# Loading 216 extra weight rows with four plain two-dimensional transfers instead of one three-dimensional one

## The chip, the cores and the metric

The kernel runs on one core of one Trainium2 chip. The metric is the device time of one launch in microseconds (us). Each comparison below was run in rounds on one chip: the kernel under test and the kernel before in turn. Runs of the kernel before scatter between 1334.8 and 1335.7 us over the chips used, and within one set of rounds on one chip by 0.2 to 0.8 us, so a few tenths of a microsecond are at the edge of what can be seen.

## The reference, cut to what matters

Two branches work on the same two rows `x` (two batch rows, one position, 1024 wide). Branch A is attention over a long cache, branch B a small mixing network. The result is a gated sum.

```python
# A: 32 heads, 16384 cached positions, head size 128, bf16: 2 x 268 MB of cache are read once
q = (x @ wq) per head;  p = softmax(q @ k_cache^T * 128**-0.5);  a = (p @ v_cache) @ wo
# B
h  = gelu(layernorm(x) @ w1)
hs = shifted(h) @ w2            # shifts along the sequence, zero padded
x1 = x + hs;  b = x1 + gelu(layernorm(x1) @ w3) @ w4
out = g * a + (1 - g) * b
```

The sequence has one position, so every shifted block of `h` is padding: `shifted(h)` is all zeros and `hs` is zero. The kernel still loads all of `w2` (1024 x 1024 bf16, 2 MB) and multiplies it by a tile of zeros.

## The kernel before

K and V are loaded in 8 MB pieces (two heads each) into a ring of three buffers, always from the SP queue. The small weights take a turn in the same ring. `w1` and `w2` share one turn, issued about 204 us into the run.

```python
    WAYS, QUAD, BASE, MORE = 3, 4, 6, 18
    W2_MORE = slice(0, WAYS * QUAD)                      # partitions 0 to 11
    n_more = WAYS * QUAD * MORE                          # 216 rows, 432 KB
    n_rest = D - P * BASE - n_more                       # 40 rows
    W2_REST = slice(64, 64 + n_rest)
    W2_ROWS = ( [(slice(0, P), r) for r in range(BASE)]
        + [(W2_MORE, BASE + r) for r in range(MORE)]
        + [(W2_REST, BASE)] )

    def load_w1_w2():
        t = load_rows(["w1"], [B_w1])
        w2 = t[:, KC * D : (KC + BASE + MORE) * D].rearrange("p (r n) -> p r n", n=D)
        nc.sync.dma_start(                               # six rows on each of 128 partitions
            out=w2[:, 0:BASE, :], in_=B_w2[0 : P * BASE, :].rearrange("(p r) n -> p r n", p=P)
        )
        r0 = P * BASE
        nc.sync.dma_start(                               # 18 more rows on each of partitions 0 to 11
            out=w2[W2_MORE, BASE : BASE + MORE, :],
            in_=B_w2[r0 : r0 + n_more, :].rearrange("(y x r) n -> x y (r n)", x=WAYS, y=QUAD),
        )
        r0 += n_more
        nc.sync.dma_start(out=w2[W2_REST, BASE, :], in_=B_w2[r0:D, :])   # 40 rows
    # ... cut ...
    def half_rows(key, actT, slots):                     # one matmul per slot and half
        for n, (rows, r) in enumerate(slots):
            for g in range(2):
                nc.tensor.matmul(ps[group(g), :], lhsT=actT[rows, r, :],
                    rhs=w[rows, r, g * HW : (g + 1) * HW], ...)
```

So `w2` is not spread evenly: 256 of its rows are taken from the even share and 216 of them put on 12 partitions.

Of the kernel before, what the change touches and what calls it, by code (L numbers as in the profile page):

```python
# [23 lines left out]
def kernel(  # L24
# [15 lines left out]
    nc = tc.nc  # L40
# [84 lines left out]
    WAYS, QUAD, BASE, MORE = 3, 4, 6, 18  # L125
    W2_MORE = slice(0, WAYS * QUAD)
    n_more = WAYS * QUAD * MORE
# [9 lines left out]
# [3 lines that stand above are left out]
        nc.sync.dma_start(  # L140
            out=w2[:, 0:BASE, :], in_=B_w2[0 : P * BASE, :].rearrange("(p r) n -> p r n", p=P)
        )
        r0 = P * BASE
        nc.sync.dma_start(
            out=w2[W2_MORE, BASE : BASE + MORE, :],
            in_=B_w2[r0 : r0 + n_more, :].rearrange("(y x r) n -> x y (r n)", x=WAYS, y=QUAD),
        )
        r0 += n_more
        nc.sync.dma_start(out=w2[W2_REST, BASE, :], in_=B_w2[r0:D, :])
        wt["w2"] = w2  # L150

    def load_rows(keys, srcs):

        t = big_tile("wt")
        c0 = 0
        for key, src in zip(keys, srcs):
            R, N = src.shape[0] // P, src.shape[1]
            v = t[:, c0 : c0 + R * N].rearrange("p (r n) -> p r n", n=N)
            nc.sync.dma_start(out=v, in_=src.rearrange("(p r) n -> p r n", p=P))
            wt[key] = v  # L160
            c0 += R * N
        return t
# [18 lines left out]
    def load_first():  # L181
# [12 lines left out]
        out=perm[:].rearrange("k (h a) -> k h a", a=4),  # L194
        in_=ident_f[:].rearrange("k (a h) -> k h a", a=4),
# [26 lines left out]
    for g in range(1, 4):  # L222
        nc.vector.tensor_tensor(
            out=osel_f, in0=osel_f, in1=ident_f[:, 40 * g : 40 * g + 8], op=ALU.add
# [9 lines left out]
        out=pick[:], in_=ident_f[:].rearrange("p (g w) -> p g w", w=32)[:, :, 0:B]  # L234
# [395 lines left out]
    def st_down():  # L630
# [5 lines left out]

    extra = {
        NT // 8: (load_w1_w2, st_mix),
        NT // 4: (lambda: load_rows(["w3"], [B_w3]), st_up),
    }  # L640
# [44 lines left out]
    for b, queue in enumerate((nc.sync, nc.scalar)):  # L685
        queue.dma_start(
            out=out[b].rearrange("s (g n) -> (s g) n", g=NQ), in_=rows[b : 96 + b + 1 : 32, :]
# [31 lines left out]
```

## Time and profile before

| what | value | view |
|---|---|---|
| device time | 1334.93 us (1334.92 to 1335.04, 3 runs) | times |
| bytes from HBM | 572.5 MB, 429 GB/s over the span | queue part of the page |
| DMA engines busy | 99.4% on the one hardware queue | queue part of the page |
| PE / DVE busy | 60% / 57% | busy part of the page |
| a 64 KB packet of K or V on one engine | 2.418 us | packets in the trace |
| one K or V load (8 such packets per engine) | lands every 19.33 us, mid-run | semaphore landings in the trace |

From the page of the kernel before: busy time, the row of 40 slices for the DMA engines (tenths, 9 is 90% or more), what they moved, the queue of the loads and the one that brings instructions (packets, MB, share of 16 engines' span), and the chain of waits by engine.

```profile
PE 797.4 (60%) x4974; PEld 351.3 (26%) x5037; DVE 760.1 (57%) x999; ACT 27.2 (2%) x68; POOL 12.8 (1%) x40
...
DMA  9999999999999999999999999999999999999998
GB/s 410 437 439 417 439 431 437 423 433 433 438 432 435 429 427 439 439 437 427 429 437 431 439 431 439 429 431 437 429 435 433 439 431 429 435 432 437 429 422 338
...
q1 hardware_dynamic: 12729, 572.54, 99.4%
q8 instruction: 39, 0.64, 0.2%
...
DVE 30%; PE 30%; DMA 23%; another core or an unknown queue 12%; issue 2%; ACT 1%; SPq 0%; ACTq 0%
```

Two parts of this page seem to disagree. The chain of waits gives DVE and PE 30% each, but the DMA engines are never idle. The chain follows what released the *issue* of each load (a buffer that PE or DVE had to free). A load that is issued while others are still queued starts no earlier for being issued earlier: the extra rows are issued by 206.1 us, and their first packet starts at 243.4 us. Here the DMA row and the GB/s row decide: the kernel is bound by the transfers.

The second view is the timeline of SP, which issues the loads, around `w1` and `w2` (start, duration, queue and line, output from input). L159 is `w1`, L140 the six even rows, L144 the extra rows, L149 the 40 rows, L108 a K load and L119 a V load.

```profile
199.62 0.33 SPq L119 DMA_DIRECT2D Vn<-in_A_v_cache_dram  x1
204.37 0.33 SPq L159 DMA_DIRECT2D wt<-in_B_w_dram  x1
204.74 0.43 SPq L140 DMA_DIRECT2D wt<-in_B_w_dram  x1
205.22 0.91 SPq L144 DMA_DIRECT2D wt<-in_B_w_dram  x1
206.17 0.39 SPq L149 DMA_DIRECT2D wt<-in_B_w_dram  x1
238.22 0.35 SPq L108 DMA_DIRECT2D Kn<-in_A_k_cache_dram  x1
242.97 0.33 SPq L119 DMA_DIRECT2D Vn<-in_A_v_cache_dram  x1
258.40 0.33 SPq L108 DMA_DIRECT2D Kn<-in_A_k_cache_dram  x1
```

SP is idle between these lines. All four loads of `w1` and `w2` are issued by 206.6 us, and the data of the extra rows lands only at 249.7 to 249.9 us: they spend most of that in the queue behind V.

The third view is a table of busy time in short stretches of the same region. The last two columns are the mean busy share of the DMA engines and GB/s; in a short stretch the share can read over 1.00, and then it only says that packets were in flight throughout.

```profile
core 0: us, PE busy (x) PEld busy (x) DVE busy (x) ACT busy (x) POOL busy (x), PEclk, DMA share, GB/s
242.00:246.00 4.00, 1.88 (x26) 1.15 (x18) 1.86 (x7) 0.00 (x0) 0.00 (x0) 0.99 1.25 488
246.00:250.00 4.00, 2.75 (x14) 1.05 (x15) 2.21 (x11) 0.78 (x2) 0.70 (x1) 0.50 1.03 422
250.00:254.00 4.00, 4.00 (x25) 1.18 (x21) 1.23 (x2) 0.00 (x0) 0.00 (x0) 0.66 1.05 446
...
256.60:260.40 3.80, 3.02 (x38) 1.75 (x34) 1.22 (x2) 0.00 (x0) 0.00 (x0) 0.89 1.03 449
```

While the extra rows are moved (243 to 250 us) the rate stays above 420 GB/s.

### The profile page before, as it was taken

The page shows a single profiled execution, that of the slowest core. Times are in us where ns is not written, and L with a number is a line of the kernel's source. Part 1 is how long each engine was busy: PE and PEld are TensorE (multiplying, and loading weights), DVE is VectorE, ACT ScalarE, POOL GpSimd, SP SyncE. Part 2 cuts the span into 40 slices and gives each one's busy share as a digit, 9 for nine tenths or more (in the row PEclk, how much of TensorE's full clock was granted, in tenths as well). Part 3 has the DMA queues.
Part 4 walks back from the last instruction along what each step waited for, and adds up shares of the span by engine and source line. Part 5 has one row for each costly group of instructions (what it writes and reads, how often), then busy time and mean ns, then how long its engine had stood idle before and what let it go on. Part 6 is the DMA issues. An engine that isn't in the chain of part 4 may idle for free.

```text
span 1333.6 us, 11483 instructions
## 1 busy us (share of the span) xinstructions
PE 797.4 (60%) x4974; PEld 351.3 (26%) x5037; DVE 760.1 (57%) x999; ACT 27.2 (2%) x68; POOL 12.8 (1%) x40
## 2 busy tenths in 40 slices
PE   2576655766556755556665555576655556665564
PEld 0223222322225322222222222232222222222231
DVE  1677665466653665555666555566655556665540
ACT  0000000000000000000000000000000000000000
POOL 0000000000000000000000000000000000000000
PEclk9788777787777777788887777888777788877775
DMA  9999999999999999999999999999999999999998
GB/s 410 437 439 417 439 431 437 423 433 433 438 432 435 429 427 439 439 437 427 429 437 431 439 431 439 429 431 437 429 435 433 439 431 429 435 432 437 429 422 338
DMA packets 12787, 573.27 MB, mean 430 GB/s; under 512 B 1797, under 2 KB 1805, under 8 KB 2613
## 3 DMA queue, kind: packets, MB, share of 16 engines
q1 hardware_dynamic: 12729, 572.54, 99.4%
q8 instruction: 39, 0.64, 0.2%
q14 instruction: 11, 0.09, 0.0%
q10 hardware_dynamic: 8, 0.00, 0.0%
HBM read 572.53 MB, written 0.00 MB: 429 GB/s over the span
## 4 chain that ended last, share of the span: by engine, by line
DVE 30%; PE 30%; DMA 23%; another core or an unknown queue 12%; issue 2%; ACT 1%; SPq 0%; ACTq 0%
DVE T L369 24%; PE S L383 19%; DMA Kn<-in_A_k_cache_dram 13%; PE O L427 7%; DMA wt<-in_B_w_dram 4%; DMA Vn<-in_A_v_cache_dram 3%; DMA wo<-in_A_wo_dram 3%; PE misc L254 2%; DVE Os L442 2%; ACT Pr L411 1%; DVE PT L415 1%; PE misc L585 1%; DVE mx L404 1%; PE misc L566 1%
## 5 line engine op out<-in xcount | busy, mean ns | idle before, releaser
L383 PE MATMUL S<-T,z 128*128 128x512 bf16 x1985 | 579.8, 419 | 330.1 <-DVE T L369 308.5
L369 DVE STREAM_TRANSPOSE T<-Kn 128x1024 f32<-128x1024 f32 x512 | 612.1, 1230 | 255.0 <-DMA Kn<-in_A_k_cache_dram 204.8
L383 PEld LDWEIGHTS <-z 128*128 128x128 bf16 x2048 | 210.0, 104 | 686.6 <-issue 522.8
L427 PE MATMUL O<-Vn,PT 128*32 128x512 bf16 x2048 | 121.4, 390 | 3.6 <-DMA Vn<-in_A_v_cache_dram 3.6
L427 PEld LDWEIGHTS <-PT 128*32 128x32 bf16 x2048 | 73.9, 141 | 49.9 <-issue 20.7
L438 DVE TENSOR_SCALAR Os<-O,xmask 128x128 f32<-128x128 f32 x32 | 11.2, 351 | 101.6 <-PE O L427 101.6
L254 PE MATMUL misc<-rs,ones_f 128*128 128x2 f32 x64 | 17.9, 349 | 79.1 <-DVE rs L458 79.1
L411 ACT ACTIVATE Pr<-S,nb 128x512 bf16<-128x512 f32 x32 | 22.0, 687 | 1199.6 <-DVE nb L406 1161.7
L394 DVE TENSOR_REDUCE m<-S 128x1 f32<-128x512 f32 x32 | 22.2, 693 | 36.9 <-PE S L383 36.9
L450 PE MATMUL misc<-asel,Os 128*128 128x2 f32 x64 | 12.2, 261 | 51.1 <-DVE Os L442 51.1
L415 DVE STREAM_TRANSPOSE PT<-Pr 128x512 bf16<-128x512 bf16 x32 | 22.8, 711 | 28.7 <-ACT Pr L411 28.7
L254 PEld LDWEIGHTS misc<-rs,ones_f 128*128 128x128 f32 x64 | 16.1, 312 | 84.0 <-issue 81.2
L442 DVE SCALAR_TENSOR_TENSOR Os<-O,xmask,Os 128x128 f32<-128x128 f32 x96 | 33.7, 351 | 3.4
L450 PEld LDWEIGHTS misc<-asel,Os 128*128 128x128 f32 x64 | 9.5, 188 | 65.3 <-DVE Os L442 61.0
L254 PE MATMUL misc<-mdiag,ones_f 128*128 128x128 f32 x64 | 15.5, 325 | 17.1 <-DVE mdiag L397 17.1
L404 DVE TENSOR_REDUCE mx<-misc 64x1 f32<-64x64 f32 x64 | 14.2, 222 | 19.1 <-PE misc L254 18.6
L343 POOL TENSOR_TENSOR z<-qsel,own 128x32 bf16<-128x32 bf16 x32 | 10.7, 335 | 1201.2 <-PE S L383 1171.4
L585 PE MATMUL misc<-xn2T,wt 128*128 128x2 bf16 x224 | 14.4, 202 | 7.3 <-DMA wt<-in_B_w_dram 7.3
L462 DVE RECIPROCAL rinv<-misc 128x2 f32<-128x2 f32 x32 | 5.5, 171 | 22.7 <-PE misc L254 22.7
L684 DVE CAST T<-out_acc 128x256 bf16<-128x256 f32 x1 | 0.4, 425 | 30.6 <-PE out_acc L476 30.6
L311 PE MATMUL misc<-wt,xT 128*2 128x512 bf16 x64 | 5.8, 541 | 19.6 <-DVE xT L299 19.6
L585 PEld LDWEIGHTS <-wt 128*128 128x128 bf16 x224 | 14.3, 172 | 7.5 <-DMA wt<-in_B_w_dram 7.5
(86 smaller groups left out, 117.7 us busy)
## 6 DMA issues: line engine op xcount, KB each, us to landing
Vn<-in_A_v_cache_dram SPq DMA_DIRECT2D x2, 4096.0 KB, 41.7
wt<-in_B_w_dram SPq DMA_DIRECT2D x1, 7168.0 KB
w<-in_B_w_dram SPq DMA_DIRECT2D x4, 1792.0 KB, 31.8
wo<-in_A_wo_dram SPq DMA_DIRECT2D x6, 1024.0 KB, 34.1
wt<-in_B_w_dram SPq DMA_DIRECT2D x1, 2048.0 KB, 37.6
wt<-in_B_w_dram SPq DMA_DIRECT2D x1, 1536.0 KB, 41.4
wo<-in_A_wo_dram SPq DMA_DIRECT2D x2, 512.0 KB, 18.8
wo<-in_A_wo_dram SPq DMA_DIRECT2D x4, 256.0 KB, 13.7
```

The costliest lines, as they stand in the source:

```text
L254: nc.tensor.matmul(ps[:], lhsT=ones_f[:], rhs=src, start=True, stop=True)
L369: moved = nc.vector.transpose(out=T[:].rearrange("p w j s -> p j w s"), in_=Kw[:, m * CW : (m + 1) * CW].rearrange("p (j w e) -> p j w e", ...
L383: nc.tensor.matmul(S[:], lhsT=z[:, v, NM - 1 - m : NM - 1 - m + P], rhs=Tb[:, v // 2, :, v % 2], start=(m == 0 and v == 0), stop=(m == NM ...
L394: nc.vector.reduce_max(out=m[:], in_=S[:], axis=AX.X)
L404: nc.vector.reduce_max(out=mx[pa, :], in_=mall[pa, pa], axis=AX.X)
L411: nc.scalar.activation(out=Pr[:], in_=S[:], func=ACTF.Exp, bias=nb[:], scale=scale, accum_out=rs[:])
L415: nc.vector.transpose(out=PT[:], in_=Pr[:])
L427: nc.tensor.matmul(O[32 * g : 32 * g + 32, :], lhsT=PT[:, m : CJ * 32 : 16], rhs=V[:, j0 : j0 + 4, :], start=(m == 0), stop=(m == NM - 1),)
L442: nc.vector.scalar_tensor_tensor(out=Os[:], in0=Ox, scalar=xmask[:, x : x + 1], in1=Os[:], op0=ALU.mult, op1=ALU.add,)
L450: nc.tensor.matmul(oc[:], lhsT=Os[:], rhs=asel[:], start=True, stop=True)
L566: nc.tensor.matmul(ps[group(g), :], lhsT=actT[rows, r, :], rhs=w[rows, r, g * HW : (g + 1) * HW], start=False, stop=(n == len(slots) - 1), ...
L585: nc.tensor.matmul(ps[:, c, :], lhsT=w[:, r, :].rearrange("k (p c) -> k p c", c=C)[:, :, c], rhs=actT[:, r, :], start=(r == 0), stop=(r == ...
```

## The change

The intent is to replace a transfer whose source has three dimensions by four whose two sides are plain: three partitions, four apart, 36 KB contiguous on each. As a side effect the rows are permuted among the 12 partitions, which changes nothing here (they meet zeros).

```diff
         r0 = P * BASE
-        nc.sync.dma_start(
-            out=w2[W2_MORE, BASE : BASE + MORE, :],
-            in_=B_w2[r0 : r0 + n_more, :].rearrange("(y x r) n -> x y (r n)", x=WAYS, y=QUAD),
-        )
+        more = B_w2[r0 : r0 + n_more, :].rearrange("(x y r) n -> x y r n", x=WAYS, y=QUAD)
+        for y in range(QUAD):
+            nc.sync.dma_start(
+                out=w2[y : WAYS * QUAD : QUAD, BASE : BASE + MORE, :], in_=more[:, y]
+            )
         r0 += n_more
```

## The prediction

> **What bounds the kernel now.** The DMA engines. The page's slice row shows them at 9 or more tenths in every slice but the last; the queue part puts 99.4% of 16 engines' span on the one hardware queue; 572.5 MB over 1333.6 us is 429 GB/s. PE (60%) and DVE (57%) have room. A K or V load is eight 65,536-byte packets per engine, 2.418 us each in the trace (19.34 us); mid-run, loads land every 19.33 us, so a load's completion adds no gap.
>
> **What the change does.** The same 432 KB of w2 go to the same 12 partitions, only permuted among them (they meet a zero left operand, so the result is unchanged).
> - Engines. [...] the load's semaphore jumps at 206.5 us, then gets exactly three landings (249.7, 249.9, 249.9), and there are twelve packets of 36,864 bytes, median 1.458 us: four per engine. [...] I expect the same three engines, four packets each, to the same partitions [...].
> - Added: three issues on SP. The old one took 0.91 us, its neighbours 0.39 to 0.43; so about 1.6 us, +0.7 us on a sequencer that mostly waits. Nine more completion packets of 9 ns, three per engine: 0.03 us.
> - Moved: loads take completion semaphores in rotation of eight. Compared instruction by instruction, PE, DVE, ACT and POOL keep their order; on SP the semaphores shift by three. The 40-row load gains a wait for the K load issued at 166.2 us, which lands at 217.8: it issues some 11 us later, but the V load ahead of it streams until 237.1. The next K load gains a wait for that V load (237.1), the next V load one for w1 (242.0); their old waits ended at 238.2 and 243.0, so 1 us of margin each, with other loads queued anyway. The tail's waits keep their distance of eight.
>
> **On the critical path.** None of it, apart perhaps from hundredths of a microsecond on three engines. In the chain of waits PE works on w1 and w2 from 248 to 258 us; the extra rows land at 249.9, while PE is on w1 (until 252), so they gate nothing. If the four loads used other engines, the effect is bounded: those three carry 144 KB more each; spread over 16 that is 27 KB, about 1 us at 2.418 us per 64 KB (an estimate). At the end four engines finish some 5 us ahead of the other twelve (landings of the wo pieces), so a shift could move the end by about 1 us either way.
>
> **Prediction: 1335.0 us, 1334.2 to 1335.9 us** (8 in 10). Faster by over 2%: 0.005; within 2%: 0.99; slower by over 2%: 0.005.
>
> **What would show it.** Right: still twelve 36,864-byte packets of about 1.4 us; three landings for each of the four loads; the lag of about 4 us of three engines in the next K load's landings (264.0 to 266.0 for thirteen, 269.6 to 269.7 for three) unchanged; the 40-row load issued near 218 us; the next K and V loads still near 238 and 243; DMA busy 99%. Wrong: another spread of those landings, smaller packets, or a drop in the DMA row near 240 us.
>
> **What would make it wrong.** Other engines; packets cut otherwise; the new waits ending later than the old and draining the queue; run-to-run differences above the 0.12 us of before's runs.

The trace of the kernel before shows three landings for its own load, and nothing of the new four. 1335.0 us is the time before (1334.93 us) with hundredths of a microsecond for the added completions, and nothing for the issues and the waits.

## The result, and the profile after

| | before | after |
|---|---|---|
| median, us | 1334.89 (1334.84 to 1335.04, 6 runs) | 1335.08 (1334.96 to 1335.37, 6 runs) |
| ratio | | 1.0002, 95% interval 0.9989 to 1.0014 |
| packets of 36,864 bytes | 12, median 1.458 us | 12, median 1.364 us |
| landings per transfer of extra rows | 3 | 3, 3, 3, 3 |
| issue of the extra rows on SP | 0.91 us | 2.92 us |

A ratio here and below is the mean time of one kernel's fast runs over that of the other's fast runs of the same rounds, so it is not quite the ratio of the medians quoted beside it.

The page of the kernel after, the same lines but that of the instruction queue, which is unchanged:

```profile
PE 804.3 (60%) x4974; PEld 353.6 (27%) x5037; DVE 760.0 (57%) x999; ACT 27.2 (2%) x68; POOL 12.8 (1%) x40
...
DMA  9999999999999999999999999999999999999998
GB/s 410 439 435 423 435 435 433 427 434 431 438 430 439 435 417 439 439 437 435 425 435 429 439 435 435 431 429 439 431 431 433 439 433 429 433 433 437 433 420 337
...
q1 hardware_dynamic: 12738, 572.54, 99.4%
...
PE 32%; DVE 29%; DMA 23%; another core or an unknown queue 12%; issue 2%; ACT 1%; SPq 0%; ACTq 0%
```

Nine packets more (12738 against 12729), all of 4 bytes (1418 against 1409 of these in the traces, 9 ns in the median), are the completions of three more transfers on three engines each. PE is 7 us busier, and the chain gives it 2% more; nothing came of either, because PE is not what the kernel waits for (`omit` below tests this).

SP's timeline after (line numbers from L144 on are one higher, L146 the four transfers, L150 the 40 rows):

```profile
199.66 0.33 SPq L119 DMA_DIRECT2D Vn<-in_A_v_cache_dram  x1
204.40 0.33 SPq L160 DMA_DIRECT2D wt<-in_B_w_dram  x1
204.78 0.42 SPq L140 DMA_DIRECT2D wt<-in_B_w_dram  x1
205.25 2.92 SPq L146 DMA_DIRECT2D wt<-in_B_w_dram  x4
217.63 0.33 SPq L150 DMA_DIRECT2D wt<-in_B_w_dram  x1
238.29 0.36 SPq L108 DMA_DIRECT2D Kn<-in_A_k_cache_dram  x1
243.03 0.33 SPq L119 DMA_DIRECT2D Vn<-in_A_v_cache_dram  x1
260.39 0.33 SPq L108 DMA_DIRECT2D Kn<-in_A_k_cache_dram  x1
```

The 40-row load is issued 11 us later (217.63 us), as its new semaphore wait asks. The next K and V loads are issued at 238.29 and 243.03 us, within 0.1 us of before. The K load after them is 2.0 us later (260.39 against 258.40), because PE finished with `w2` later. The stretches show why:

```profile
242.00:246.00 4.00, 1.88 (x26) 1.21 (x18) 1.82 (x6) 0.00 (x0) 0.00 (x0) 1.00 1.16 470
246.00:250.00 4.00, 2.76 (x14) 1.01 (x16) 2.25 (x11) 0.78 (x2) 0.70 (x1) 0.54 1.03 422
250.00:254.00 4.00, 4.00 (x25) 1.28 (x21) 1.17 (x2) 0.00 (x0) 0.00 (x0) 0.61 1.08 463
...
256.60:260.40 3.80, 3.75 (x18) 0.84 (x14) 0.60 (x2) 0.00 (x0) 0.00 (x0) 0.50 1.03 449
```

In the last stretch the granted TensorE clock was 0.50, against 0.89 before, and the matmuls on the extra rows there took 0.63 us each instead of 0.37. This is not the change's doing as far as the runs show: in `after_again`, the changed kernel run once more, the clock in that stretch was 0.73 and the K load was issued at 257.93 us. It did not cost the kernel anything: the transfers run at 449 GB/s in both.

Landings are increments of a transfer's semaphore, read from the trace, and are taken here as one per DMA engine: a K load has 16, as many as the page counts engines, and the load of extra rows in the kernel before has three, with packets that start in threes (243.44 to 243.56, 244.98 to 245.11 us and so on). Those of the K load that follows `w2`, sorted, in us:

```
before  264.0 264.0 264.1 264.1 264.4 265.2 265.3 265.5 265.5 265.6 265.7 265.7 266.0 | 269.6 269.7 269.7
after   263.9 263.9 263.9 264.0 264.1 265.1 265.2 265.2 265.2 265.2 265.3 265.3 265.6 | 269.1 269.1 269.1
```

Thirteen engines go on with K at once, and three are about 4 us late, since they carried the extra rows. After the change the pattern is the same.

### The profile page after: what moved, and what is told of

The parts are those of the page before. It is cut to its first block, busy times and chain, and to the rows that moved or that the text cites. A ratio compares the mean times of both kernels' runs of the same rounds, so it can differ in the third digit from the quotient of the medians.

```text
span 1333.4 us, 11488 instructions
## 1 busy us (share of the span) xinstructions
PE 804.3 (60%) x4974; PEld 353.6 (27%) x5037; DVE 760.0 (57%) x999; ACT 27.2 (2%) x68; POOL 12.8 (1%) x40
## 3 DMA queue, kind: packets, MB, share of 16 engines
q1 hardware_dynamic: 12738, 572.54, 99.4%
## 4 chain that ended last, share of the span: by engine, by line
PE 32%; DVE 29%; DMA 23%; another core or an unknown queue 12%; issue 2%; ACT 1%; SPq 0%; ACTq 0%
DVE T L370 23%; PE S L384 20%; DMA Kn<-in_A_k_cache_dram 13%; PE O L428 7%; DMA wt<-in_B_w_dram 4%; DMA Vn<-in_A_v_cache_dram 3%; DMA wo<-in_A_wo_dram 3%; PE misc L255 2%; DVE Os L443 2%; ACT Pr L412 1%; DVE PT L416 1%; PE misc L586 1%; PE misc L567 1%; DVE mx L405 1%
```

## The experiments

Theory A, the one of the prediction: each DMA engine carries the same bytes in the same order, and the extra issues, completions and waits fall where other loads are queued. The rivals are that the split has a small real cost (B), that only the sum of bytes matters (C), that the form of the transfer matters (D), and that waits on the issuing queue never matter (E). Two more, F and G, arose after the first four runs.

| kernel | median, us | before, same rounds | ratio (95%) |
|---|---|---|---|
| after_again | 1334.88 | 1334.96 | 1.0000 (0.9987 to 1.0012) |
| plain12 | 1340.44 | 1334.96 | 1.0048 (1.0036 to 1.0061) |
| omit | 1334.74 | 1334.96 | 0.9998 (0.9985 to 1.0012) |
| split8 | 1339.47 | 1334.96 | 1.0034 (1.0020 to 1.0047) |
| step1 | 1341.13 | 1334.98 | 1.0045 (1.0032 to 1.0059) |
| spread8 | 1337.63 | 1334.98 | 1.0019 (1.0006 to 1.0033) |
| even8 | 1335.28 | 1334.98 | 1.0003 (0.9990 to 1.0015) |
| split5 | 1335.05 | 1334.98 | 1.0000 (0.9985 to 1.0016) |
| step32 | 1340.35 | 1335.24 | 1.0038 (1.0023 to 1.0053) |
| spread8b | 1336.26 | 1335.24 | 1.0008 (0.9991 to 1.0025) |

All gave the right result. In `omit`, `spread8`, `spread8b` and `step32` matmuls on `w2` are left out, and the result is right only because they multiply zeros. By the 2% measure all ten are "the same"; the differences that matter here are of 1 to 6 us against a scatter of some tenths.

### after_again: the changed kernel once more

No edit.

> The changed kernel once more, for the size of the difference. Theory A (each DMA engine carries the same bytes in the same order; the extra issues, completions and waits fall where other loads are queued): within 0.3 us of the kernel before, and the +0.2 us of the first six runs (1335.08 against 1334.89) may shrink to nothing or stay, as nothing of the change works 0.2 us into the end. Rival B (the split costs something small that reaches the end): +0.2 us or more again, every run above every run of before.

Measured: 1334.88 us (1334.85 to 1335.10, 5 runs) against 1334.96 us (1334.78 to 1335.07, 9 runs). The 0.2 us of the first rounds did not come back, so B has no support; it is not excluded below some tenths of a microsecond.

### split5 and split8: when do the added waits cost something?

Loads take their completion semaphores in rotation from eight (in the trace of `before` all landings are on eight semaphores, which load after load takes in turn), so a load waits until the load eight places before it has landed: in `after` the 40 rows are issued at 217.63 us, and that load, a K load, has its last landing at 217.62 us. The change makes the `w1`/`w2` turn seven loads instead of four. These two kernels go on in the same direction.

```diff
 # split8 (against the changed kernel): eight transfers of 9 rows; split5: only y == 0 is cut in two
         for y in range(QUAD):
-            nc.sync.dma_start(
-                out=w2[y : WAYS * QUAD : QUAD, BASE : BASE + MORE, :], in_=more[:, y]
-            )
+            for h in range(0, MORE, 9):
+                nc.sync.dma_start(
+                    out=w2[y : WAYS * QUAD : QUAD, BASE + h : BASE + h + 9, :],
+                    in_=more[:, y, h : h + 9],
+                )
```

> Eight transfers of 9 rows instead of the changed kernel's four of 18; same engines, same bytes. Now the rotation of eight semaphores is used up by w2 itself: the seventh and eighth wait for w1 and the six base rows to land (242.0 and 246.1 us in before), the 40-row load for the first of the eight, and the next K load for the second, so it is issued near 247.5 us, not 238.2. Theory A: the queue of thirteen engines runs dry from about 244 to 246 until about 248.5, and the time grows by 2 to 4 us (1337 to 1339 us), with that gap in the landings. Rival E (waits of the issuing queue never matter because the buffers hold enough): within 0.3 us of the changed kernel.

> Five transfers: one of the changed kernel's four cut in two halves. The next K load now waits for w1 to land (242.0 us) instead of the V load before (237.1), and the V load after it for the six base rows (246.1). The queue holds work until 243.4 us at the earliest, so theory A expects the K load issued near 242 us, 4 us later than in before, and no cost: within 0.4 us. If the cost of the split to eight (+4.5 us) were one of issues or completions by number rather than of a drained queue, a quarter of the added transfers would cost about a quarter of it, +1.1 us.

Measured: split5 1335.05 us, no cost. split8 1339.47 us, +4.5 us, a little over the 2 to 4 us expected. SP's timeline of split5 and then of split8:

```profile
237.04 0.33 SPq L152 DMA_DIRECT2D wt<-in_B_w_dram  x1
241.93 0.36 SPq L108 DMA_DIRECT2D Kn<-in_A_k_cache_dram  x1
245.80 0.33 SPq L119 DMA_DIRECT2D Vn<-in_A_v_cache_dram  x1
```

```profile
205.19 40.97 SPq L147 DMA_DIRECT2D wt<-in_B_w_dram  x8
246.20 0.44 SPq L152 DMA_DIRECT2D wt<-in_B_w_dram  x1
246.76 0.35 SPq L108 DMA_DIRECT2D Kn<-in_A_k_cache_dram  x1
247.21 0.37 SPq L119 DMA_DIRECT2D Vn<-in_A_v_cache_dram  x1
```

In split5 the next K load is issued at 241.93 us, 3.7 us later than before, and nothing is lost, since the six even rows of `w2` land only from 243.6 us on: the queue still had work. In split8 the K load is issued at 246.76 us, when most engines have run dry; its first packets start at 247.8 us. The stretch of split8 shows the hole (before: 1.25 and 488 GB/s):

```profile
242.00:246.00 4.00, 1.88 (x31) 1.04 (x23) 1.82 (x6) 0.00 (x0) 0.00 (x0) 1.00 0.60 255
```

So E is wrong: waits on the issuing queue do matter, at a threshold, here between an issue at 241.93 us and one at 246.76 us. The cost does not go with the number of transfers (five cost nothing, eight cost 4.5 us); it begins when the last wait ends after the queue has run empty. The changed kernel is on the free side: its next K load waits for a V load that lands at 236.9 us, and is issued at 238.29 us, as before. In the profiled runs, whose spans are 4.2 us apart (1337.8 and 1333.6 us), the last K load landed on its latest engine 3.1 us later than before (1257.2 against 1254.1 us), so some 1.1 us was added after that. Among the last loads the latest engine drops 1.4 us further behind (it lands at 1321.7 us, the next latest at 1320.3) just after a packet of instructions starts (1318.9 us); `omit` below shows more of these packets. That it was this packet is read from the timing alone.

### omit: do the 432 KB cost anything at all?

```diff
 # against the kernel before
-        nc.sync.dma_start(
-            out=w2[W2_MORE, BASE : BASE + MORE, :],
-            in_=B_w2[r0 : r0 + n_more, :].rearrange("(y x r) n -> x y (r n)", x=WAYS, y=QUAD),
-        )
 ...
-        + [(W2_MORE, BASE + r) for r in range(MORE)]
```

> The 432 KB are not loaded and their 36 matmuls left out (the result stays right only because their left operand is zero for one position). Theory A: the three engines run about 5.6 us earlier after w2 (four packets of 1.36 to 1.46 us), the other thirteen carry what they did; if those set the end, the time stays within 0.3 us of before, and if the three loaded ones were the last by a little, it falls by at most 0.5 us. Rival C (bandwidth of the sum): 432 KB less at 430 GB/s, so -1.0 us. Also if PE mattered here, 8 us of its work less would show: theory A says it does not.

Measured: 1334.74 us (1334.60 to 1334.97) against 1334.96 us: -0.2 us, hardly above the scatter, where C asked for -1.0; C is out. PE had 36 matmuls less, and the K load that waits for PE's work on `w2` was issued at 253.51 us instead of 258.40, also without effect. The landings of the last K load (its 16 engines, us) say why:

```
before 1246.8 1246.8 1247.0 1247.4                      | 1252.3 1252.3 1252.5 1252.6 1252.8 1252.9 1253.0 1253.7 1253.9 1253.9 1254.1 1254.1
omit   1246.5 1246.5 1246.6 1246.6 1247.0 1247.0 1247.1 | 1252.2 1252.4 1252.4 1252.5 1253.3 1253.4 1253.5 1253.6 1253.7
```

The 16 engines do not keep step. Without the extra rows seven of them are about 6 us ahead of the other nine by 1250 us. With the extra rows four are ahead and three have joined the nine: 144 KB each (four packets, together 5.7 us after the change and 5.9 before) is about what those three had to spare. The uneven layout of `w2` puts bytes on engines that would otherwise wait for the rest at the end.

No run was made to find why nine engines fall behind, but the traces show something of it. The page lists 39 packets (16,384 bytes each in the trace; 0.88 to 1.03 us each) on a queue of kind "instruction" (q8). In `even8` (below), where every load is spread evenly, the lag of the 16 engines behind the first of them, summed, grew by 0.2 us on average from one K or V landing to the next when no such packet started in between (25 stretches of 19.33 us), and by 1.2 us when one did (28 stretches; those with the few packets of the smaller instruction queue are left out). After the first of these packets one engine is more than 0.85 us late, from 283 us on there are nine, and it stays at nine to the end of the cache loads. So the nine late engines seem to be those that carry instruction packets too. The trace does not name engines and no run changed these packets, so this rests on the timing alone; why it is nine stays open.

### even8: the even layout

```diff
 # against the kernel before; the load of extra rows, the 40-row load and their slots removed
-    WAYS, QUAD, BASE, MORE = 3, 4, 6, 18
+    WAYS, QUAD, BASE, MORE = 3, 4, 8, 0
```

> w2 as eight rows on each of 128 partitions in one transfer: no extra rows, 16 matmuls instead of 50. The run without extra rows showed seven fast and nine slow engines, 6 us apart at the end, with the end set by the nine. Theory A: here every one of the nine carries 24 to 32 KB more than before (0.9 to 1.2 us at 2.418 us per 64 KB), so +0.7 to +1.3 us, about 1335.9 us, although PE has 7 us less to do and one or two fewer transfers are issued. Rival C (sum of bytes): 0.0; a rival in which issues or PE count: below before.

Measured: 1335.28 us (1335.18 to 1335.79) against 1334.98 us, +0.3 us and inside the interval of "no difference". The sign is as expected, the size is a third of it. On the nine late engines the last K load landed at 1252.7 to 1254.1 us, no later than before (to 1254.1), and 0.4 us later than in `omit` (to 1253.7). So bytes per engine are not the whole account: some of what the nine gain in bytes they seem to have lost before in another way. In the kernel before, the 65,536-byte packets of other engines that started beside the extra rows took up to 2.8 us rather than 2.418, which would go that way: between 243 and 250 us their median was 2.63 us, while none of `even8` in that stretch took longer than 2.418. That this makes up the difference is only argued. A miss of my estimate, left open.

### plain12: one plain transfer of 12 partitions

```diff
 # against the kernel before
-            in_=B_w2[r0 : r0 + n_more, :].rearrange("(y x r) n -> x y (r n)", x=WAYS, y=QUAD),
+            in_=B_w2[r0 : r0 + n_more, :].rearrange("(p r) n -> p r n", r=MORE),
```

> The same 432 KB to the same 12 partitions in the changed kernel's row order, as one plain two-dimensional transfer of 12 partitions. Theory A [...]: 12 engines with one 36,864-byte packet each, so twelve landings; three engines lose 108 KB, nine gain 36 KB (1.36 us at the trace's packet time); the 4 us lag of three engines in the next K load's landings goes away. The end moves by what the latest engines gained: +0.5 to +1.4 us, 1335.4 to 1336.3 us. Rival C (only the sum of bytes matters): 0.0 us. Rival D (the form of the transfer, not the engines, matters): like the changed kernel, three landings.

Measured: 1340.44 us (1340.24 to 1343.76), +5.5 us; expected were +0.5 to +1.4. The number of engines was as expected: twelve landings, one 36,864-byte packet each (so not the three of D, and the time rules out the 0.0 of C). But each packet took 2.99 to 4.56 us instead of 1.4 to 1.6, and 65,536-byte packets of other loads beside them took up to 7.4 us. Stretches of plain12 (columns as before):

```profile
242.00:246.00 4.00, 1.88 (x26) 1.19 (x18) 1.81 (x6) 0.00 (x0) 0.00 (x0) 1.00 1.26 279
246.00:250.00 4.00, 2.75 (x14) 1.10 (x14) 2.25 (x11) 0.78 (x2) 0.70 (x1) 0.64 1.34 214
250.00:254.00 4.00, 4.00 (x22) 1.48 (x20) 1.08 (x2) 0.00 (x0) 0.00 (x0) 0.51 0.75 268
```

The busy share reads 1.26 and 1.34, while the rate falls from 422 to 214 GB/s in the second stretch. Packets in flight count as busy, also when they are held up. A full DMA row alone is therefore no proof that the transfers run at speed; the GB/s row has to be read beside it.

Neither theory A nor its rivals had this. Apart from the number of engines, what differs is the partitions that are written at once. In plain12 it is twelve neighbouring partitions, 0 to 11, with a landing for each. In the kernel after it is three partitions four apart in each transfer, with three landings. In the kernel before it should be the same three, since its transfer splits the 12 partitions into three runs of four, but that is inferred: the trace counts landings and names neither engines nor partitions. That it matters which partitions are written at once is theory F; the rival G is that many engines in one short transfer are slow whatever the partitions.

### step1: the same engines and bytes, other partitions

```diff
 # against the changed kernel
-        more = B_w2[r0 : r0 + n_more, :].rearrange("(x y r) n -> x y r n", x=WAYS, y=QUAD)
+        more = B_w2[r0 : r0 + n_more, :].rearrange("(y x r) n -> x y r n", x=WAYS, y=QUAD)
 ...
-                out=w2[y : WAYS * QUAD : QUAD, BASE : BASE + MORE, :], in_=more[:, y]
+                out=w2[WAYS * y : WAYS * (y + 1), BASE : BASE + MORE, :], in_=more[:, y]
```

> Four plain transfers as in the changed kernel, but each to three neighbouring partitions (0 to 2, 3 to 5, 6 to 8, 9 to 11) instead of three partitions four apart: same engines, bytes, packets, issues and waits; only which engine writes which partition differs. Theory F [...]: the twelve packets take 2 to 3 times 1.36 us, the extra rows land 4 to 8 us later than 250 us, other engines' packets near 245 to 255 us lengthen as in the one transfer of 12 partitions (where they took up to 7 us), and the time grows by 2 to 8 us. Rival A (only engine and bytes count): within 0.3 us of before, packets of 1.4 to 1.6 us.

Measured: 1341.13 us (1340.99 to 1341.26), +6.15 us, worse than plain12. The packets took a median of 2.87 us (1.45 to 3.39), and the fourth transfer landed at 254.2 to 257.4 us instead of 249.2 to 249.4. The last K load's three latest engines land at 1258.6, 1258.8 and 1260.1 us, the latest in the kernel before at 1254.1. Stretches of step1:

```profile
246.00:250.00 4.00, 2.76 (x13) 1.34 (x15) 2.25 (x11) 0.78 (x2) 0.71 (x1) 0.61 1.03 358
250.00:254.00 4.00, 4.00 (x23) 1.28 (x20) 0.69 (x2) 0.00 (x0) 0.00 (x0) 0.54 1.03 338
```

This is the same number of transfers, engines, bytes and packets as in the changed kernel, with the same waits. Where the bytes are written, only the step between the partitions differs: one instead of four. The rows read at once also lie closer in HBM (36 KB apart instead of 144), but the kernel before reads them just so, and `spread8` below too, with packets of 1.36 to 1.69 us, so it is not that. Theory A as it stood is not enough: the partitions that are written at once belong in it.

### step32: partitions 32 apart

```diff
 # against the changed kernel; matmuls on the extra rows and on the 40 rows left out
-    W2_REST = slice(64, 64 + n_rest)
+    W2_REST = slice(68, 68 + n_rest)
 ...
-                out=w2[y : WAYS * QUAD : QUAD, BASE : BASE + MORE, :], in_=more[:, y]
+                out=w2[y : 96 : 32, BASE : BASE + MORE, :], in_=more[:, y]
```

> The changed kernel's four transfers, but with the three partitions 32 apart (y, 32+y, 64+y); the 40 rows moved to partitions 68 to 107, and the 38 matmuls on both left out (result right only because the left operand is zero). Theory F [...]. Packets of two of the engines take about twice 1.36 us, the extra rows land near 254 to 256 us, and the time grows by 3 to 6 us. Rival (only neighbouring partitions disturb each other): packets of 1.4 to 1.6 us, within 0.4 us of before.

Measured: 1340.35 us (1340.27 to 1340.40), +5.1 us. Packets took 2.08 to 2.89 us and the last of the extra rows landed at 255.0 to 255.1 us. So partitions of one transfer need not be neighbours for its packets to be slow, and the rival is out. The expectation had two slow engines, but the packets came in threes of nearly equal length, so all three were slow alike. Which property of the partitions makes it so is not shown: this is one layout, and steps other than 1, 4 and 32 were not tried. Unlike in step1, the other engines were held as much: their 65,536-byte packets that started between 240 and 257 us took a median of 4.3 us (2.85 in step1), the rate fell to 194 GB/s, and the next K load landed about 5 us later on all engines (269.2 to 271.0, and 274.5 for the three).

```profile
246.00:250.00 4.00, 2.75 (x15) 1.22 (x16) 2.25 (x11) 0.78 (x2) 0.70 (x1) 0.70 0.95 194
250.00:254.00 4.00, 3.35 (x25) 1.03 (x21) 1.79 (x4) 0.00 (x0) 0.00 (x0) 0.88 0.92 242
```

Why the other engines were held too, no run here shows.

### spread8 and spread8b: eight engines, partitions four apart

```diff
 # against the kernel before, in place of its load of extra rows; matmuls on these rows left out
+        more = B_w2[r0 : r0 + n_more, :].rearrange("(p r) n -> p r n", r=MORE)
+        nc.sync.dma_start(out=w2[0:32:4, BASE : BASE + MORE, :], in_=more[0:8])
+        nc.sync.dma_start(out=w2[1:16:4, BASE : BASE + MORE, :], in_=more[8:12])      # spread8
 # spread8b has in place of the last line
+        nc.sync.dma_start(out=w2[1:8:4, BASE : BASE + MORE, :], in_=more[8:10])
+        nc.sync.dma_start(out=w2[2:8:4, BASE : BASE + MORE, :], in_=more[10:12])
```

> The same bytes as 12 partitions' rows, one transfer to partitions 0, 4, ... 28 and one to 1, 5, 9, 13: eight engines[...] (36 matmuls on the extra rows left out; as in the kernel without them, the result stays right only because the left operand is zero). Theory F: packets stay at 1.36 to 1.6 us, so the number of engines alone does not cost what the one transfer of 12 partitions cost (+5.5 us); what is left is the bytes on slow engines[...], so 0.5 to 1.6 us over before. Rival G (more engines in one short transfer are slow whatever the partitions): +4 us or more and packets of 3 us or more.

> As in the kernel with eight engines [...]. [...] the time grew by 2.65 us, which is what two 36,864-byte packets take (2.72 us) [...]: theory A expects half the loss, +1.0 to +1.6 us. If the loss came from the number of engines or of transfers instead: again +2.5 us or more.

The sums: for spread8 one packet (1.36 us) more on each of five engines, for spread8b half of spread8's 2.65 us, with at most one packet more on an engine that may be late. They are estimates.

Measured: the packets stay fast in both (medians 1.369 and 1.430 us, at most 1.69), so G is out: eight engines at once are no trouble when the partitions of each transfer are four apart. The times grow by 2.65 us (spread8, expected 0.5 to 1.6) and 1.0 us (spread8b, expected 1.0 to 1.6). The first expectation was careless: the second transfer of spread8 writes four partitions, and if four of the eight engines carry it, three of them those that carried the extra rows before, a fourth gets two packets, 72 KB, not one. The kernel before suggests that small loads share engines: of the ten landings of its 40 rows seven come by 246.7 us and three at 250.4 to 250.5 us, just after the extra rows (249.7 to 249.9). If the fourth engine is one of the nine late ones, two packets of 1.36 us (2.72 us) are just the loss; with at most one packet for such an engine, spread8b lost 1.0 us, somewhat under half. This is an estimate: the trace does not show which engines they were. (The 95% interval of spread8b includes no difference, but each of its four runs is above all seven of the kernel before.) In spread8 a single engine lands the last K load last, at 1256.6 us, 2.5 us behind the latest one before. By this estimate, what a late engine is given was paid almost in full in spread8 (2.65 of 2.72 us), to about three quarters in spread8b and to a third in even8; what three of the early ones were given (`omit`) was nearly free.

## Why the prediction was right

- **The size.** 1335.0 us was predicted, 1335.08 us measured, inside 1334.2 to 1335.9. A repeat gave 1334.88 us.
- **Bound by the transfers.** Held. PE's work on `w2` ended 2 us later in the changed kernel and 5 us earlier in `omit`, and neither moved the time.
- **Same engines, same packets.** Held: twelve packets of 36,864 bytes, three landings for each of the four transfers, thirteen landings of the next K load at 263.9 to 265.6 us and three at 269.1. Landings counted elsewhere: three for 12 partitions from a source of three dimensions (before), twelve for twelve (plain12), eight for eight (spread8), ten for 40 (before). The number expected for the four transfers came out; these counts do not show that it holds in general.
- **The same partitions for each engine.** The prediction said it in half a sentence and rested nothing on it. The runs showed that the partitions written at once carry the result: the same four transfers to neighbouring partitions cost 6.15 us. That the change left this as it was (for the kernel before it is inferred) is, for the argument, luck.
- **Three more issues.** The direction held, the size was off: four issues were put at 4 x 0.4 = 1.6 us and took 2.92 us (0.64 to 0.85 each). The neighbours from which 0.4 us was read write partitions one apart; in step1, where the four transfers do so too, they took 1.27 us together (0.24 to 0.35 each). The rows of step1 also follow each other in HBM, but so do those of spread8b, whose transfers to two partitions four apart took 0.56 and 0.59 us each. So the issue of these transfers takes longer when the partitions are not neighbours (at 32 apart, in step32, it is 0.64 to 0.85 us again). SP is idle then, and it cost nothing.
- **The added waits.** Held, with the margin as read: the 40 rows issued at 217.63 us (near 218 predicted), the next K and V loads at 238.29 and 243.03 us (near 238 and 243). split5 and split8 show how much room there was: 4 us later costs nothing, 8.5 us later costs 4.5 us.
- **The bound on being wrong.** "If the four loads used other engines ... about 1 us" was wrong as a bound. The estimate counted bytes per engine averaged over 16, and left out that nine engines run behind the other seven (about 6 us by 1250 us in `omit`) and that the partitions which are written at once matter. Other engines cost up to 5.5 us (plain12), other partitions 5.1 and 6.15 us (step32, step1), and even with partitions four apart and fast packets, spread8 cost 2.65 us. The change happened to keep the number of engines and the step between the partitions, so this did not bear on its time.

No version that the experiments point to is clearly faster: leaving the load out altogether was worth about 0.2 us, and nothing done to these rows alone can be expected to do better.

## What to carry to other kernels

When a transfer is rewritten in a kernel bound by transfers, ask three things: how many engines carry it, which partitions are written at once, and whether the queue still holds work when the waits it adds have ended; here all three stayed, and the form of the transfer was free. For a transfer to a few partitions, try partitions four apart: here three of them at once were free (packets of 1.36 us, +0.2 us), three neighbours cost 6.15 us and three 32 apart 5.1 us. And read the GB/s row beside the DMA busy row: held-up packets count as busy (a share of 1.34 beside 214 GB/s in plain12).
